# Pieces of 384 tokens, joined rows of array tiles and blocks of 1024 tokens in a two-stage feed-forward kernel on one core

## The chip, the cores and the metric

The kernel runs on one core of one Trainium2 chip. The metric is the device time of one execution in microseconds (us), and the time of a kernel is the median of its runs.

## The reference, cut to what matters

Eight batches of 576 tokens, 8 heads of 64. A packed attention (32 learned queries read the keys and values, then the tokens read the 32 results) gives x of 4608 x 512. Two feed-forwards follow, all in float32.

```python
p_packed = sm_attn(p, k, v)                 # 32 rows per head
out = sm_attn(q, p_packed, p_packed)        # 576 rows per head
x = out.transpose(0, 2, 1, 3).reshape(4608, 512)
h = x @ w_in                                # 512 x 2048
x = (h * sigmoid(1.702 * h)) @ w_out        # 2048 x 512
h = max(x @ w1, x @ w2, x @ w3)             # 512 x 768 each
return h @ w_out2                           # 768 x 512
```

## The kernel before

**Precision.** Every large product is made of three matmuls (`mm3`, lines 111 to 115): each operand is kept as a high and a low part of the reduced type fp32r, and low x high, high x low and high x high are added up in one PSUM bank. Each of the three has weights of its own to load.

**First feed-forward.** For a batch and a group of four heads, the second attention product and `w_in` are put together: `pw_unit` multiplies the 32 packed rows of each head with their rows of `w_in`, so that h is the attention weights `at` times `pw`. These are matmuls of 64 rows by 32 columns, 8 of which stand in the array side by side; in float32 each is issued as two instructions, so a row of one group (g) for two batches is 16 instructions on line 460. The two results go through the two banks of `ps_a`, and ScalarE and VectorE split them into high and low parts (lines 146 and 147). The work is then cut into units: 288 tokens (half a batch, `HALF`) by 128 of the 2048 inner columns (`fc`). `h_unit` has 2 x 3 matmuls into one of the two banks of `ps_h`, then the activation; `g_unit` splits the result; `out_unit` has 4 x 3 matmuls that are summed over `fc` in the four banks of `ps_c`. A batch half takes 16 units, then its result goes to `x2d` in DRAM. Batches 0 and 1 take their halves in turns of 4 and 8 columns (`PAT`), with partial sums kept in SBUF; of the other batches only the last does (chunks of 4).

**Second feed-forward.** Six blocks of 768 tokens. A 2 x 2 block product with seven multiplications (Strassen's form) is made for each of nine weight sets (three weights, three pairs of column blocks): `Set.steps` has seven products of 2 x 3 matmuls with 384 columns, and VectorE adds them up and takes the maximum. The sums of x (T1 to T4) and their splits are made once a block by `x_steps`, from what `x_loads` brings; the weight sets come from DRAM with two loads each (`load_set`, lines 664 and 665, issued on POOL), where earlier steps (`Piece`) have put them. `out2` then multiplies by the last weights: 18 matmuls of 512 columns for 128 tokens.

**Order.** `main` writes down a due time for every step (`add`), sorted into one program order. The framework then orders the instructions of each engine by that order and by when their operands and buffers are ready. `tn[n]` is the due time of unit n; `pw_unit` of a pair of batches stands `Q_` or `R_` units ahead of its first use. Buffers come from pools: 16 large ones (`wp`, tag "w") for weights, x and weight sets, and 4 (tag "x") for the first feed-forward's results and the reloaded `w_in` parts (`load_wi`).

## Time and profile before

| | us |
|---|---|
| median of 3 runs | 1297.01 |
| lowest and highest run | 1295.29, 1297.29 |
| the profiled execution | 1295.06 |
| its span, first to last instruction | 1293.3 |
| TensorE busy in the span | 1272.8 (98%) |
| VectorE, ScalarE, POOL busy | 841.8, 522.7, 78.2 |
| moved by DMA | 233.07 MB |

All times inside the kernel are those of the one profiled execution. Matmuls overlap each other, so the busy time of a group of matmuls counts parts of the span more than once, and the distance between two starts is what one of them takes. A line in square brackets behind an instruction tells how long its engine had been idle and what released it.

### The profile page before, as it was taken

The numbers are of one execution on the slowest core, as the hardware profiler recorded it, in microseconds if no ns is written. First come the engines' busy times: TensorE is split into PE (matmuls) and PEld (weight loads), VectorE is DVE, ScalarE is ACT, GpSimd is POOL, SyncE is SP. The second block draws the span as 40 slices with busy tenths as digits, with TensorE's granted clock in tenths as the row PEclk, the third lists the DMA queues.
The fourth block names the chain that finished last, engine by engine and source line by source line (L and its number), as shares of the span: only waits on it lengthen the run. The fifth ranks groups of instructions, "written<-read, shape, count | busy, mean of one in ns | idle before, by whom it ended". The sixth has DMA issues, their size and how long they took to land.

```text
span 1293.3 us, 24741 instructions
## 1 busy us (share of the span) xinstructions
PE 1272.8 (98%) x9990; PEld 1179.7 (91%) x9990; DVE 841.8 (65%) x1734; ACT 522.7 (40%) x1133; POOL 78.2 (6%) x153
## 2 busy tenths in 40 slices
PE   6999999999999999999999999999999999999998
PEld 5688888899989899999999999899899999998997
DVE  7998788565543466588789887557467366366561
ACT  3676654454654454455556532312213123113111
POOL 1000000000000000000000011011011011010100
PEclk8999999999999999999999999999999999999999
DMA  8898254323220231045557399567477477474541
GB/s 311 315 406 314 74 157 145 103 88 99 91 87 18 90 109 48 24 145 182 170 180 240 129 347 342 202 218 245 157 260 250 156 260 247 160 254 177 187 172 49
DMA packets 84402, 233.07 MB, mean 180 GB/s; under 512 B 9792, under 2 KB 38976, under 8 KB 77376
## 3 DMA queue, kind: packets, MB, share of 16 engines
q1 hardware_dynamic: 64128, 115.62, 26.0%
q0 software_dynamic: 20160, 115.88, 25.8%
q8 instruction: 78, 1.28, 0.4%
q14 instruction: 36, 0.29, 0.1%
HBM read 191.88 MB, written 39.58 MB: 179 GB/s over the span
## 4 chain that ended last, share of the span: by engine, by line
PE 88%; DVE 5%; DMA 3%; ACT 2%; issue 1%; SPq 0%; DVEq 0%; ACTq 0%
PE p L115 10%; PE p L114 10%; PE p L113 10%; PE acc L113 10%; PE acc L115 9%; PE acc L114 9%; PE h L113 5%; PE h L115 4%; PE h L114 4%; PE accb L115 4%; PE accb L114 4%; PE accb L113 4%; PE pw L460 2%; PE s L311 1%; DMA wraw_o<-in_w_out 1%; PE pv L366 1%
## 5 line engine op out<-in xcount | busy, mean ns | idle before, releaser
L113 PE MATMUL acc<-g,wo 128*128 128x288 f32 x1024 | 309.0, 302 | 1.9 <-DVE x L559 1.4
L115 PE MATMUL acc<-g,wo 128*128 128x288 f32 x1024 | 301.1, 294 | 0.0
L114 PE MATMUL acc<-g,wo 128*128 128x288 f32 x1024 | 299.4, 292 | 0.0
L113 PEld LDWEIGHTS acc<-g,wo 128*128 128x128 f32 x1024 | 192.2, 188 | 32.3 <-ACT t L526 11.9
L115 PEld LDWEIGHTS acc<-g,wo 128*128 128x128 f32 x1024 | 192.0, 188 | 1.4 <-issue 1.3
L114 PEld LDWEIGHTS acc<-g,wo 128*128 128x128 f32 x1024 | 192.3, 188 | 0.6 <-issue 0.5
L113 PE MATMUL h<-at,pw 128*128 128x288 f32 x512 | 154.0, 301 | 1.2 <-ACT at L142 0.6
L114 PE MATMUL h<-at,pw 128*128 128x288 f32 x512 | 151.5, 296 | 0.4 <-DVE at L143 0.4
L115 PE MATMUL h<-at,pw 128*128 128x288 f32 x512 | 151.3, 296 | 0.0
L113 PE MATMUL p<-x_T,ws 128*128 128x384 f32 x324 | 108.2, 334 | 0.0
L114 PE MATMUL p<-x_T,ws 128*128 128x384 f32 x324 | 108.2, 334 | 0.0
L115 PE MATMUL p<-x_T,ws 128*128 128x384 f32 x324 | 108.1, 334 | 0.0
L750 DVE TENSOR_TENSOR u<-s,p 128x384 f32<-128x384 f32 x54 | 29.9, 554 | 118.3 <-PE p L115 118.3
L113 PEld LDWEIGHTS h<-at,pw 128*128 128x128 f32 x512 | 96.1, 188 | 9.7 <-issue 5.0
L534 DVE TENSOR_TENSOR g<-t,g 128x288 fp32r<-128x288 f32 x130 | 58.9, 454 | 67.9 <-ACT g L533 67.0
L524 ACT ACTIVATE t<-h 128x288 f32<-128x288 f32 x130 | 53.3, 410 | 112.5 <-PE h L115 112.1
L114 PEld LDWEIGHTS h<-at,pw 128*128 128x128 f32 x512 | 96.1, 188 | 1.6 <-DVE t L527 0.8
L115 PEld LDWEIGHTS h<-at,pw 128*128 128x128 f32 x512 | 96.1, 188 | 0.5 <-issue 0.5
L780 ACT COPY s<-p 128x384 f32<-128x384 f32 x54 | 25.9, 480 | 164.5 <-PE p L115 164.5
L527 DVE SCALAR_TENSOR_TENSOR t<-t,h 128x288 f32<-128x288 f32 x126 | 56.8, 451 | 54.1 <-ACT t L526 53.4
L526 ACT ACTIVATE t<-h 128x288 f32<-128x288 f32 x126 | 51.8, 411 | 93.2 <-PE h L115 92.7
L115 PE MATMUL accb<-wo,g 128*128 128x512 f32 x216 | 84.1, 390 | 0.0
(166 smaller groups left out, 2587.7 us busy)
## 6 DMA issues: line engine op xcount, KB each, us to landing
ws<-wss POOLq DMA_DIRECT2D x54, 1024.0 KB, 7.5
wa<-wsa POOLq DMA_DIRECT2D x54, 768.0 KB, 4.6
wi<-wsc POOLq DMA_DIRECT2D x24, 512.0 KB, 3.7
k<-in_k SPq DMA_DIRECT2D x16, 576.0 KB, 4.0
q<-in_q SPq DMA_DIRECT2D x16, 576.0 KB, 4.1
x2d<-x SPq DMA_DIRECT2D x16, 576.0 KB, 3.6
wss<-ws SPq DMA_DIRECT2D x36, 256.0 KB, 2.9
xr<-x2d SPq DMA_DIRECT2D x24, 384.0 KB, 4.3
```

The lines of the kernel that those rows point to most:

```text
L113: nc.tensor.matmul(o, al, bh, start=start, stop=False, skip_group_check=more)
L114: nc.tensor.matmul(o, ah, bl, start=False, stop=False, skip_group_check=more)
L115: nc.tensor.matmul(o, ah, bh, start=False, stop=stop, skip_group_check=more)
L311: self.mm = nc.tensor.matmul(o[hf][rows(c, r, hf ^ self.swap), :HALF], w(c, rows_in(r)), x[rows_in(r), c, hf * HALF:hf * HALF + HALF], sta ...
L366: self.mm = nc.tensor.matmul(o[h][m, :D], self.et[rows_in(h), c * P + NP * j:c * P + NP * j + NP], self.v[rows_in(h), c, d:d + D], start=c ...
L460: nc.tensor.matmul(os[b][rows(x, r, b & 1)], sp[b, g][rows_in(r), NP * c:NP * c + NP], w[rows_in(r), c], start=True, stop=True,)
L524: latest["act"] = nc.scalar.activation(t, o, AF.Gelu_apprx_sigmoid)
L526: nc.scalar.activation(t, o, AF.Tanh, scale=0.5 * 1.702)
L527: nc.vector.scalar_tensor_tensor(out=t, in0=t, scalar=1.0, in1=o, op0=ALU.add, op1=ALU.mult)
L534: latest["dve"] = nc.vector.tensor_tensor(out=g[:, 1], in0=gt[n], in1=f(g[:, 0]), op=ALU.subtract)
L750: latest["dve"] = nc.vector.tensor_tensor(out=o, in0=a, in1=b, op=op)
L780: latest["act"] = nc.scalar.copy(self.s1, self.b1)
```

## The change

In the first feed-forward, batches 2 to 7 are taken as one run of 3456 tokens in 9 pieces of 384. A piece may lie across two batches; its `h_unit` then computes h in two parts of 192 columns. The last two pieces are interleaved in chunks of four inner column blocks. The result of a piece is stored in two halves. The rows of both groups are computed one directly behind the other (`pw_both`), the second into the banks of `ps_h`, and the output unit of the piece before is moved from behind the next `h_unit` to directly behind the rows. Where this happens follows from the due times (three pairs of batches 0 and 1 and all twelve of batches 2 to 7).

The second feed-forward takes three blocks of 1024 tokens and two of 768, so a product has 512 or 384 columns. For blocks after the first, `x_loads` and `x_steps` run twice, for one half of the rows (k) each, through smaller buffers. A third of the weight sets from number 11 on have buffers of their own, sets 2 to 10 are loaded one set later than before, a third of the split results g moves to the large buffers, and there are fewer m, t and g buffers. The tables of due times are replaced.

```diff
-BT = 768
-HT = BT // 2
-NBLK = NT // BT
+HTS = [512, 512, 512, 384, 384]
+HT = max(HTS)
+NBLK = len(HTS)
+C0 = [2 * sum(HTS[:j]) for j in range(NBLK)]
+WIDE = 384
...
-T_ = [41.76, 1.21, 1.17, 7]
+T_ = [40.26, 1.21, 1.17, 10]
...
-    def pw_unit(bs, pr, g, n):
+    def pw_unit(bs, pr, g, n, tile_=pa_tile):
...
-            os[b] = pa_tile(f"pw_{b}_{g}_{n}")
+            os[b] = tile_(f"pw_{b}_{g}_{n}")
...
+        return lambda: pw_out(os, g, n)
...
+    def pw_both(bs, pr, n):
+        for done in [pw_unit(bs, pr, g, n, (pa_tile, h_tile)[g]) for g in range(2)]:
+            done()
...
+    runs = [(x, 0, NFC) for x in range(2 * S, NT, WIDE)]
+    runs[-2:] = [(x, y, y + 4) for y in range(0, NFC, 4) for x in range(NT - 2 * WIDE, NT, WIDE)]
...
     def h_unit(n):
...
+        for b, t0, num, to in parts:
+            for g in range(2):
+                w = pw[b, fc // 4][:, g]
+                mm3(
+                    o[:, to:to + num], (w[:, 0, fs], w[:, 1, fs]), [t[:, t0:t0 + num] for t in at[b, g]],
+                    g == 0, g == 1, len(parts) > 1,
+                )
...
     def load_set(n):
...
+        if n > 9 and n % 3 == 2:
+            a = late["x"].tile([P, 12 * P], F32R, tag="wa", name=f"wa_{n}")
+            s_ = late["x"].tile([P, 16 * P], F32R, tag="ws", name=f"ws_{n}")
...
-                st[key] = f_tile("m", 8, f"m_{self.n}_{c}")
+                st[key] = f_tile("m", 6, f"m_{self.n}_{c}", self.ht)
...
+                add(tn[nn] + hu[nn] / 2 + .02, pw_both, (2 * pr, 2 * pr + 1), pr, n)
+                early.add(nn - 1)
+
+        for n in range(N1):
+            add(tn[n], h_unit, n)
+            add(tn[n + 1] + hu[n + 1] / 2 + .03 if n in early else tn[n + 2] + hu[n + 2] / 2, out_unit, n)
+            add(tn[n] + hu[n] / 2 + .01, g_unit, n)
...
+            elif n < 11:
+                add(max(ts[n - 2] + DS[0] * 6 / 7 + .1, saved.get(n, 0)), load_set, n)
             else:
                 add(ts[n - 2] + .1, load_set, n)
...
-                add(t0 - 14, x_loads, j + 1)
-                for dt, fn in x_steps():
-                    add(t0 + 1 + 1.5 * dt, fn)
+                add(t0 - 14, x_loads, j + 1, 0)
+                add(t0 + .9, use_x, j + 1)
+                for dt, fn in x_steps(0):
+                    add(t0 + 1 + E_[0] * dt, fn)
+                add(t0 + 1 + E_[0] * 9.1, open_raw, j + 1, 1)
+                add(t0 + 1 + E_[0] * 9.1 + .1, x_loads, j + 1, 1)
+                for dt, fn in x_steps(1):
+                    add(t0 + E_[1] * DO[j] + E_[0] * dt, fn)
```

## Rows read from the trace of the kernel before

**Rows 1.** The page's head: span, busy time and share of each engine

```profile
span 1293.3 us, 24741 instructions
PE 1272.8 (98%) x9990; PEld 1179.7 (91%) x9990; DVE 841.8 (65%) x1734; ACT 522.7 (40%) x1133; POOL 78.2 (6%) x153
```

**Rows 2.** Busy by stage: stretch, length, engines (instructions), clock, DMA share, GB/s

```profile
260.00:620.00 360.00, 359.95 (x3495) 332.09 (x3494) 210.21 (x486) 181.45 (x431) 7.55 (x14) 1.00 0.28 91
620.00:749.00 129.00, 128.39 (x972) 127.94 (x971) 108.33 (x244) 73.24 (x160) 2.70 (x5) 1.00 0.53 178
749.00:1293.30 544.30, 540.67 (x2919) 514.85 (x2917) 314.38 (x576) 124.45 (x223) 55.53 (x103) 1.00 0.62 217
```

**Rows 3.** Timeline of TensorE (start, duration, instruction): first and last of 361 matmuls

```profile
623.67 0.30 PE L113 MATMUL h<-at,pw 128*128 128x288 f32 x1
...
671.15 0.30 PE L113 MATMUL h<-at,pw 128*128 128x288 f32 x1
```

**Rows 4.** The same timeline, second feed-forward: ends of 43 matmuls, then of 87

```profile
1020.38 0.33 PE L113 MATMUL p<-x_T,ws 128*128 128x384 f32 x1
...
1027.66 0.33 PE L113 MATMUL p<-x_T,ws 128*128 128x384 f32 x1
...
1269.79 0.39 PE L113 MATMUL accb<-wo,g 128*128 128x512 f32 x1
...
1289.29 0.39 PE L115 MATMUL accb<-wo,g 128*128 128x512 f32 x1
```

**Rows 5.** Groups by line: count | busy us, mean ns | idle before

```profile
L460 PE MATMUL pw<-wi,sp 64*32 64x512 f32 x384 | 26.1, 601 | 0.0
```

**Rows 6.** Timeline of the weight loads behind a pair of 64-column matmuls

```profile
291.84 0.32 PEld L383 LDWEIGHTS ptp<-fold,pn 128*128 128x128 f32 x2
292.08 0.19 PEld L113 LDWEIGHTS acc<-g,wo 128*128 128x128 f32 x1
292.19 0.19 PEld L114 LDWEIGHTS acc<-g,wo 128*128 128x128 f32 x1
```

**Rows 7.** Timeline of TensorE around one row of array tiles

```profile
353.81 0.29 PE L115 MATMUL h<-at,pw 128*128 128x288 f32 x1
354.02 1.09 PE L460 MATMUL pw<-wi,sp 64*32 64x512 f32 x16
355.04 0.41 PE L113 MATMUL acc<-g,wo 128*128 128x288 f32 x1
355.28 0.29 PE L114 MATMUL acc<-g,wo 128*128 128x288 f32 x1
```

**Rows 8.** Timeline of TensorE, two rows of batches 0 and 1

```profile
120.00 1.09 PE L460 MATMUL pw<-low_wi,sp 64*32 64x512 f32 x16
...
123.69 1.68 PE L460 MATMUL pw<-low_wi,sp 64*32 64x512 f32 x16 [0.82 <-DVE pw L147]
```

**Rows 9.** Timelines of VectorE and TensorE: emptying behind the row of 354.02, behind another

```profile
355.81 1.29 DVE L147 TENSOR_TENSOR pw<-pw,pw 128x512 fp32r<-128x512 f32 x2 [0.31 <-ACT pw L146]
...
616.20 1.09 PE L460 MATMUL pw<-wi,sp 64*32 64x512 f32 x16
...
619.49 1.28 DVE L147 TENSOR_TENSOR pw<-pw,pw 128x512 fp32r<-128x512 f32 x2
```

**Rows 10.** Groups by line and shape, VectorE

```profile
L750 DVE TENSOR_TENSOR m<-t,m 128x384 f32<-128x384 f32 x108 | 59.5, 555 | 2.3
L626 DVE TENSOR_TENSOR c<-c,wa 128x512 f32<-128x512 f32 x18 | 12.3, 685 | 0.0
```

**Rows 11.** POOL's timeline, one set; issues of 740 to 780: KB, median landing

```profile
770.51 0.55 POOL L664 DMA_DIRECT2D wa<-wsa  x1 [5.70 <-PE p L115]
771.55 0.54 POOL L665 DMA_DIRECT2D ws<-wss  x1 [0.49 <-PE p L115]
...
ws<-wss POOLq DMA_DIRECT2D x5, 1024.0 KB, 9.1
```

**Rows 12.** Timeline of TensorE at the start of the first feed-forward

```profile
42.37 0.40 PE L114 MATMUL h<-at,pw 128*128 128x288 f32 x1 [0.42 <-DVE at L143]
```

More of the change, by code (lines that the diff above doesn't have):

```diff
@@ L530, in g_unit @@
     def g_unit(n):
-        g = gp.tile([P, 2, HALF], F32R, tag="g", name=f"g_{n}")
+        g = gp.tile([P, 2, WIDE], F32R, tag="g", name=f"g_{n}")[:, :, :units[n][0][1]]
         if direct(n):
@@ L542, in out_unit @@
     def out_unit(n):
-        b, hf, fc = units[n]
+        (c0, width, _), fc = units[n]
         w = wo[fc]
@@ L554, in out_unit @@
             if dc == 0:
[L555 to L557 removed]
+                old = part.pop(c0, None)
+                num = KD if width == HALF else 2
+                x2 = old or [
+                    x_tile(f"x2_{n}_{y}")[:, :num * width].rearrange("p (c t) -> p c t", c=num)
+                    for y in range(KD // num)
+                ]
+            to = x2[dc // num][:, dc % num]
             if old is not None:
[L559 to L569 removed]
+                nc.vector.tensor_tensor(out=to, in0=o, in1=to, op=ALU.add)
+            elif dc % 2 == 0 or c0 < 2 * S:
+                nc.scalar.copy(to, o)
+            else:
+                nc.vector.tensor_copy(to, o)
+            if fc == NFC - 1 and dc % num == num - 1:
+                nc.sync.dma_start(x2d[:, dc + 1 - num:dc + 1, c0:c0 + width], x2[dc // num])
+        if n in last and fc < NFC - 1:
+            part[c0] = x2
     wo2, xs, xv, st = {}, {}, {}, {}
     ws = {}
+    xt = {}
     nps = [0]
+    gw = {}
     def c_tile(name):
@@ L770, in put @@
                 fc, hf = self.p + c // 2 * 3, c % 2
-                g = late["f"].tile([P, 2, HT], F32R, tag="g", bufs=12, name=f"g2_{self.n}_{c}")
+                if self.p == 0:
+                    if (self.j, fc) not in gw:
+                        gw[self.j, fc] = w_tile(f"g2_{self.n}_{fc}")
+                    g = gw[self.j, fc][:, hf, :, :self.ht]
+                else:
+                    g = late["f"].tile([P, 2, HT], F32R, tag="g", bufs=8, name=f"g2_{self.n}_{c}")[:, :, :self.ht]
                 nc.scalar.copy(g[:, 0], m)
@@ L883, in main @@
         attention(A_[3], 1, 1, AS_[3], 0)
-        N1 = 2 * B * NFC
+        N1 = len(units)
         tn = [0.0] * 300
+        early = set()
         t = T0
+        hu = [HU * (units[min(n, N1 - 1)][0][1] / HALF) for n in range(N1 + 2)]
         for n in range(N1 + 2):
             tn[n] = t
-            if n < N1:
-                add(t, h_unit, n)
-            if n >= 2:
-                add(t + HU / 2, out_unit, n - 2)
-            if n < N1:
-                add(t + HU / 2 + .01, g_unit, n)
-            t += (T_[1] * HU) if n < T_[3] else HU * T_[2]
+            t += hu[n] * (T_[1] if n < T_[3] else T_[2])
         TB0 = t
```

257 lines of the change are left out of this document (135 added, 122 removed).

## The prediction

> **What bounds the kernel now.** I read the page's head first: TensorE is busy in 1272.8 of 1293.3 us, every other engine below two thirds [rows 1]. The same engine by stage comes next [rows 2]: from 260 us to the end it is never free for more than 0.7 us in a stage until the tail, at the full clock (2.4 GHz). So in those stages nothing but the matmuls' own time counts, and a wait on another engine is a loss only if the change makes one. The price of a matmul is then not its busy time (they overlap) but the distance between starts. In a stretch without interruption the first feed-forward takes 47.48 us for 20 units of 18 matmuls of 288 columns, 131.9 ns each [rows 3]. The second takes 7.28 us for 42 matmuls of 384 columns, 173.3 ns, and 19.50 us for 86 of 512, 226.7 ns [rows 4]. At 2.4 columns per ns that is 120 + 11.9, 160 + 13.3 and 213.3 + 13.3. So what wider pieces can save is about 13 ns for each matmul that disappears.
>
> The sum is made against the profiled execution, 1295.06 us (span 1293.3 and 1.76 around it). That is 1.95 below the median of 1297.01, so what comes out is shifted by 1.95 at the end.
>
> **Wide pieces in the first feed-forward.** Batches 2 to 7 have 192 units of 18 matmuls: 3456 x 131.9 = 455.8 us. After, the same 3456 tokens are 9 pieces of 384, 144 units. Six pieces lie in one batch: 96 x 18 x 173.3 = 299.5. Three straddle two batches, and there h is computed in two halves of 192 columns, because each batch has weights of its own: 48 x 12 matmuls of 384 for the output, 99.8, and 48 x 12 = 576 of 192 for h. No matmul of 192 columns of this type is in the trace. From below it costs 80 + 13.3 = 93.3 ns, by the two wider shapes; from above 131.9, the nearest shape. What chooses is the weight load, since every one of these matmuls has its own 128x128 weights. The trace shows it uncovered at one place only: behind a pair of 64-column matmuls the starts of the following loads stand 0.11 us apart, though there is little to stream [rows 6]. The two loads of the first row (0.32 us with a last load of 0.19) start at 291.84 and 291.97; the next at 292.08 and 292.19: 0.11 and 0.11. The two other instances that I read, at 203 and 269 us, give the same, with a mean of 0.111. I take 0.111, since that is the load itself: 63.9 us. Sum 463.3 against 455.8: **+7.5 us**, between -2.7 (93.3 ns) and +19.5 (131.9). The wide pieces cost more at the seams than they save.
>
> The Trainium skill ("TensorE: Matmul & The Clock Gate", Back-to-back issue gap) puts the distance of warm matmuls at N/2.4 + 2.5 ns, which the rows here exceed by about 10 ns at every width; by it both forms would be within 1.5 us of each other, and the seams would be free. The same page's section on LDWEIGHTS has the load at columns/1.2, 107 ns for 128, which would make the seams 61.6 us; the rows side with that one.
>
> VectorE and ScalarE get fewer and longer instructions per token, and they are off the path. The last two pieces run interleaved in chunks of four, as batch 7 did.
>
> **Rows of array tiles.** The weights of two batches (pw) are now made for both groups in one go, 32 instead of 16 instructions. One row costs, from the matmul before to the second one after it, 355.28 - 353.81 = 1.47, less two matmul slots of 0.13: 1.21 us [rows 7]. The instruction lasts 0.60 us at 512 columns [rows 5] against 0.39 for the same width in the feed-forward [rows 4]: 0.21 longer, which is another 512 columns at 2.4 per ns, so these stream at half rate, 0.427 us, on 8 tiles: 0.85 for 16 instructions. The other 0.36 is paid for changing the array's form and back, once per row. Twelve merged pairs in batches 2 to 7 save 12 x 0.36 = 4.4 us. Of batches 0 and 1 three pairs are merged; there the rows also waited for their banks, as at 123.69 [rows 8]. The six rows cost 9.9 us in all by the same measure; 3 x 2.07 with a stall of 0.4 each is 7.4: -2.5.
>
> The new wait: the second group writes into the two banks of h, so the next h waits until ScalarE and VectorE have emptied them. Two tiles are empty 3.07 us after the row's start at best, at 0.64 each (355.81 + 1.29, less 354.02) [rows 9]; the third, which frees the first h bank, at 3.71. TensorE is done with the long row at 1.98 (it went on 1.13 after the short one's start, 0.85 are added) and has the output unit that was moved there in front of the next h, 12 x 173.3 = 2.08: 4.06. So in the clean case it is hidden. Where other work is queued on the two engines it isn't: at 616.20 the second tile was empty only after 4.57 (619.49 + 1.28) [rows 9], 1.5 later. Of the 24 rows in batches 2 to 7, 7 are late by 0.8 us or more. Behind the waiting h stand the next h and all output units; nobody else waits. Cost between 0 and 5 us (four pairs at 1.2); I take 2.5. The two loads of group weights that a joined row needs go out together, 10 and 8 units ahead, on POOL, which has nothing else to issue then; they share four buffers with the pieces' results, and a pair that gets its buffer late moves its row, which I cost at 0. Together **-4.4 us**.
>
> **Second feed-forward.** A set is 42 matmuls. Six blocks of 9 sets at 384 are 2268 x 173.3 = 393.1 us. After: 27 sets at 512, 1134 x 226.7 = 257.1, and 18 at 384, 131.0: 388.1. **-5.0 us**. The output part (36 tiles) keeps its matmuls. What has to stay hidden: in a last set of three VectorE has 13 instructions, 13 x 0.685 (the 512-wide row) = 8.9 in 9.52 us, where it had 13 x 0.555 = 7.2 in 7.28 [rows 10]; so cover is no thinner. The x sums come in two rounds of 11 VectorE instructions, 15.1 us, and a reload between them, within 8 x 18 x 226.7 ns = 32.6 us of output work (12.2 in 24.5 for the short blocks). SP has the second round's loads ahead of some output stores; those wait for VectorE's first round, which leaves the output copies half of the stage, and I cost it at 0. Weight sets 2 to 10 are now asked for one set ahead (9.52 us) instead of two: POOL issues the second load 1.0 us behind the first, it lands in 9.1 at this stage [rows 11], and its first reader runs 9.52 + 1.36 (one product of 6) = 10.9 after the release. 0.8 us of margin: cost 0, and up to 1 us a set if it is gone. The handover between the stages holds weights of two batches to the end of the first feed-forward, so x and set 0 get their buffers one chunk (8 units) later; I cost it at 0, at most 3 us.
>
> **Start.** Unit 0 waits for batch 0's attention until 42.37 [rows 12]; by the due times it is placed 1.5 us sooner and group 1's loads go first. The bounds are -3 and +2; I take **-1.5**.
>
> Sum: 7.5 - 4.4 - 5.0 - 1.5 = -3.4: 1291.7 for the profiled execution, **1293.6** as a median, 0.26% faster.
>
> **The rivals.** *Free seams*: the 192-column matmul costs 93.3 ns, the weight load being hidden there too. For it: at 288 columns loads do follow at 131.9 without showing. Against: rows 6. It gives 10.2 less: 1283.4. *Bank wait (slower)*: the third tile is late at most of the 15 places. If all are as at 616 us, third release 5.2 against 4.06, it is 15 x 1.15 = 17 instead of 2.5: 1308. It decides from a mean wait of 0.65 us, with which the total passes 1299.6. For it: 7 of 24 rows of before are late enough. Against: their places are moved. The skill warns of just this ("TensorEngine Tiling (Array Packing)", PSUM Bottleneck: packing speeds up TensorE but not the emptying of PSUM); the late rows agree. *Rows not joined*: the order that is issued follows readiness, and at 120.00 and 123.69 two rows that the code gives one after the other ran 3.7 us apart [rows 8]. Then the 4.4 are lost: 1298.0. *Late sets*: 9 sets x 1 us: 1302. *Half rate*: the narrow matmuls fall to the rate of rows 5, 173.3 ns: +36, 1329.5; nothing narrow contradicts it, no wide one supports it.
>
> **How the numbers follow.** Forecast 0.43, free seams 0.15, bank wait 0.20, not joined 0.10, late sets 0.08, half rate 0.04. About 0.2% (2.6 us) is what can be told from no change, so faster is below 1294.4: 0.33 of the forecast, all of free seams, 0.04 of others, 0.52. Slower (above 1299.6): 0.14 of bank wait, half rate, 0.04 of late sets, 0.22. The rest, 0.26, is within. The range goes from free seams with no bank wait (1281) to a bank wait of 0.9 us (1303), leaving half rate and the worst bank wait out. The forecast alone is 1288 to 1298.
>
> **What would show it.** The distance of the 192-column starts: 0.11, or 0.093, or 0.173. A straddling unit should take 3.4 us, a plain wide one 3.12. The rows of 32 should show one form change, and h behind them an idle time released by the pw evacuation. The second feed-forward should show 226.7 ns and no idle time at sets 2 to 10 or at the handover. I am wrong if the seams are cheap, if the two rows run apart, or if idle time sits behind them in most places.

## The result and the profile after

| | before | after |
|---|---|---|
| median, us | 1296.37 | 1307.22 |
| lowest and highest run | 1295.29, 1297.29 | 1306.72, 1308.32 |
| the profiled execution | 1295.06 | 1307.14 |
| first feed-forward ends (first product `p`) | 749.12 | 763.84 |
| last matmul ends | 1289.68 | 1301.40 |

The ratio of the runs on one chip is 1.0085 (95% interval 1.0068 to 1.0103). The change makes the kernel 0.85% slower; the forecast was 0.26% faster, and 1307.2 lies above its range. The head of the page and the busy time by stage, which answer to [rows 1, 2]; the columns are those of rows 2, with the boundary of the stages moved to 763.84:

```profile
span 1305.4 us, 22517 instructions
PE 1277.5 (98%) x9036; PEld 1141.9 (87%) x9036; DVE 835.0 (64%) x1618; ACT 510.2 (39%) x1032; POOL 68.3 (5%) x135
```

```profile
260.00:620.00 360.00, 359.54 (x3085) 332.43 (x3091) 203.55 (x430) 172.32 (x360) 8.63 (x16) 1.00 0.28 90
620.00:763.84 143.84, 138.07 (x864) 136.03 (x849) 116.61 (x238) 72.78 (x138) 2.70 (x5) 0.99 0.51 172
763.84:1305.40 541.56, 536.52 (x2539) 465.35 (x2538) 309.31 (x532) 122.88 (x221) 45.84 (x85) 1.00 0.55 187
```

The loss is not in the middle of the first feed-forward, where TensorE is as busy as it was. It is in its last stretch: 5.8 us free between 620 and 763.84, where before had 0.6, and a clock below 1.00. The matmuls' own prices first, in the timeline of TensorE (start, duration): six matmuls of 192 columns, one plain unit of 384 from its first h to the next unit's, a joined row with its neighbours, and a set of 512 columns from one product to the same product of the next set.

```profile
707.58 0.27 PE L121 MATMUL h<-at,pw 128*128 128x192 f32 x1
...
708.14 0.27 PE L123 MATMUL h<-at,pw 128*128 128x192 f32 x1
...
666.77 0.33 PE L121 MATMUL h<-at,pw 128*128 128x384 f32 x1
...
669.89 0.33 PE L121 MATMUL h<-at,pw 128*128 128x384 f32 x1
...
413.67 0.34 PE L123 MATMUL acc<-g,wo 128*128 128x384 f32 x1
413.94 1.95 PE L468 MATMUL pw<-wi,sp 64*32 64x512 f32 x32
415.81 0.44 PE L121 MATMUL acc<-g,wo 128*128 128x384 f32 x1
416.09 0.33 PE L122 MATMUL acc<-g,wo 128*128 128x384 f32 x1
...
890.60 0.39 PE L121 MATMUL p<-x_T,wa 128*128 128x512 f32 x1
...
900.12 0.39 PE L121 MATMUL p<-x_T,wa 128*128 128x512 f32 x1
```

Every price of the sum is there, as in [rows 3, 4, 7]: 0.56/5 = 0.112 for 192 columns (the mean of all such distances is 0.1110), 3.12/18 = 0.1733 for 384, 416.09 - 413.67 - 2 x 0.1733 = 2.07 for a joined row (2.07 was worked out), 9.52/42 = 0.2267 for 512. Now the stretch that nobody priced. VectorE's timeline, TensorE's, and the busy time of two stretches behind it (the granted clock stands behind POOL's column):

```profile
709.84 0.43 DVE L615 TENSOR_SCALAR c_o<-wraw_o 128x512 int32<-128x512 int32 x1 [1.15 <-DMA wraw_o<-in_w_out]
...
712.66 1.94 DVE L586 TENSOR_TENSOR x<-acc,x 128x384 f32<-128x384 f32 x4
...
713.36 0.66 PE L121 MATMUL acc<-g,wo 128*128 128x384 f32 x1 [4.95 <-DVE x L586]
```

```profile
713.30:716.70 3.40, 3.34 (x11) 3.37 (x12) 3.40 (x7) 1.04 (x3) 0.00 (x0) 0.50 0.69 249
716.80:718.00 1.20, 1.20 (x12) 1.20 (x11) 0.97 (x3) 0.00 (x0) 0.00 (x0) 1.00 0.98 227
```

After the last 192-column matmul at 708.14 TensorE has nothing to do until 713.36: the output unit needs the four output banks, and the four adds (L586) that bring the interleaved pieces' partial sums out of them stand in VectorE's queue behind conversions (L615 to L624) of the second feed-forward's last weights (`conv_wo2`), one of which waits for its raw weights. Behind the 4.95 us the clock is granted at 0.50, half of full speed (1.2 GHz), until 716.7, and at 1.00 again from 716.8. The twelve matmuls of this output unit take 3.71 us (713.36 to the next h at 717.07) where 12 x 0.1733 = 2.08 is their price: 1.6 us more. With the 5.1 us in front of them, 6.7 of the last stretch's loss stand at this one place.

For a balance, the price by its width was taken from every distance between starts of TensorE's timeline; what is left over goes to the rows, waits and other work. The waits of h behind the rows stand in the line of the other gaps.

| part | forecast | found, after less before |
|---|---|---|
| start, to the first output matmul | -1.5 | +1.6 (48.86 to 50.50) |
| first feed-forward, matmul slots | +7.5 | +7.5 (605.4 to 612.9) |
| rows of array tiles, with the wait before them | -4.4 | -4.5 (39.1 to 34.6) |
| attention's rows and transposes between units | 0 | +3.9 |
| other gaps up to 630 us | 0 | -1.4 |
| idle time and half clock from 630 us on | 0 | +7.7 (1.2 to 8.9) |
| second feed-forward | -5.0 | -3.0 (540.6 to 537.6) |
| sum | -3.4 | +11.8 |

### The profile page after: what moved, and what is told of

It is laid out like the page before. It is cut to its first block, busy times and chain, and to the rows that moved or that the text cites. A ratio compares the mean times of both kernels' runs of the same rounds, so it can differ in the third digit from the quotient of the medians.

```text
span 1305.4 us, 22517 instructions
## 1 busy us (share of the span) xinstructions
PE 1277.5 (98%) x9036; PEld 1141.9 (87%) x9036; DVE 835.0 (64%) x1618; ACT 510.2 (39%) x1032; POOL 68.3 (5%) x135
## 4 chain that ended last, share of the span: by engine, by line
PE 84%; DVE 7%; issue 3%; ACT 3%; DMA 2%; SPq 0%; POOL 0%; POOLq 0%; ACTq 0%; DVEq 0%
PE acc L121 9%; PE p L121 9%; PE p L122 9%; PE p L123 9%; PE acc L123 9%; PE acc L122 9%; PE h L121 5%; PE h L122 5%; PE h L123 5%; PE accb L123 4%; PE accb L121 4%; PE accb L122 4%; PE pw L468 2%; PE s L319 2%; PE pv L374 1%
## 5 line engine op out<-in xcount | busy, mean ns | idle before, releaser
L121 PE MATMUL acc<-g,wo 128*128 128x384 f32 (+1 forms) x832 | 273.0, 330 | 6.1 <-DVE x L586 5.2
L123 PE MATMUL acc<-g,wo 128*128 128x384 f32 (+1 forms) x832 | 268.8, 324 | 0.0
L122 PE MATMUL acc<-g,wo 128*128 128x384 f32 (+1 forms) x832 | 268.7, 323 | 0.0
L121 PEld LDWEIGHTS acc<-g,wo 128*128 128x128 f32 x832 | 156.1, 188 | 24.8 <-issue 10.1
L121 PE MATMUL h<-at,pw 128*128 128x384 f32 (+2 forms) x512 | 157.5, 308 | 2.8 <-ACT at L150 1.8
L122 PEld LDWEIGHTS acc<-g,wo 128*128 128x128 f32 x832 | 156.9, 189 | 1.7 <-DVE g L557 1.1
L123 PEld LDWEIGHTS acc<-g,wo 128*128 128x128 f32 x832 | 156.6, 188 | 0.1
L122 PE MATMUL h<-at,pw 128*128 128x384 f32 (+2 forms) x512 | 155.5, 304 | 0.0
L123 PE MATMUL h<-at,pw 128*128 128x384 f32 (+2 forms) x512 | 155.1, 303 | 0.0
L121 PEld LDWEIGHTS h<-at,pw 128*128 128x128 f32 x512 | 96.8, 189 | 13.7 <-issue 6.2
L121 PE MATMUL p<-x_T,ws 128*128 128x512 f32 (+1 forms) x270 | 99.4, 368 | 1.0 <-DMA ws<-wss 1.0
L550 DVE SCALAR_TENSOR_TENSOR t<-t,h 128x384 f32<-128x384 f32 (+1 forms) x112 | 57.2, 512 | 66.8 <-ACT t L549 66.4
L122 PE MATMUL p<-x_T,ws 128*128 128x512 f32 (+1 forms) x270 | 99.3, 368 | 0.0
L123 PE MATMUL p<-x_T,ws 128*128 128x512 f32 (+1 forms) x270 | 99.0, 367 | 0.0
L122 PEld LDWEIGHTS h<-at,pw 128*128 128x128 f32 x512 | 97.2, 190 | 1.3 <-DVE at L151 0.8
L123 PEld LDWEIGHTS h<-at,pw 128*128 128x128 f32 x512 | 97.3, 190 | 0.0
L785 DVE TENSOR_TENSOR u<-s,p 128x512 f32<-128x512 f32 (+1 forms) x45 | 28.5, 634 | 106.6 <-PE p L123 106.3
L549 ACT ACTIVATE t<-h 128x384 f32<-128x384 f32 (+1 forms) x112 | 51.5, 461 | 106.5 <-PE h L123 105.9
L557 DVE TENSOR_TENSOR g<-t,g 128x384 fp32r<-128x384 f32 (+1 forms) x96 | 50.8, 530 | 61.8 <-ACT g L556 61.6
L121 PE MATMUL accb<-wo,g 128*128 128x512 f32 x216 | 84.1, 389 | 0.0
L123 PE MATMUL accb<-wo,g 128*128 128x512 f32 x216 | 84.0, 389 | 0.0
L122 PE MATMUL accb<-wo,g 128*128 128x512 f32 x216 | 84.0, 389 | 0.0
```

What stands on the lines that cost most here:

```text
L121: nc.tensor.matmul(o, al, bh, start=start, stop=False, skip_group_check=more)
L122: nc.tensor.matmul(o, ah, bl, start=False, stop=False, skip_group_check=more)
L123: nc.tensor.matmul(o, ah, bh, start=False, stop=stop, skip_group_check=more)
L549: nc.scalar.activation(t, o, AF.Tanh, scale=0.5 * 1.702)
L550: nc.vector.scalar_tensor_tensor(out=t, in0=t, scalar=1.0, in1=o, op0=ALU.add, op1=ALU.mult)
L557: latest["dve"] = nc.vector.tensor_tensor(out=g[:, 1], in0=gt[n], in1=f(g[:, 0]), op=ALU.subtract)
```

## The experiments

All against the kernel before on the same chip. "Ends" is the start of the first product `p`, "second" the time from there to the last matmul's end. Times inside a kernel are those of its one profiled execution, which can lie up to 3 us from its median.

| kernel | median | ratio (95%) | ends | second |
|---|---|---|---|---|
| before | 1296.4 | | 749.1 | 540.6 |
| changed | 1307.2 | 1.0085 (1.0068 to 1.0103) | 763.8 | 537.6 |
| e1 pieces of 288, joined rows | 1297.9 | 1.0015 (1.0005 to 1.0026) | 754.8 | 539.4 |
| e2 pieces of 288, rows apart | 1295.6 | 0.9995 (0.9984 to 1.0006) | 751.0 | 538.8 |
| e3 no seams | 1290.0 | 0.9959 (0.9945 to 0.9972) | 736.0 | 546.4 |
| e4 adds first | 1308.6 | 1.0096 (1.0083 to 1.0109) | 760.8 | 542.7 |
| e6 light last weights | 1314.6 | 1.0146 (1.0132 to 1.0159) | 772.9 | 536.3 |
| e7 small first block | 1309.2 | 1.0101 (1.0087 to 1.0114) | 763.7 | 541.1 |
| e8 rows apart | 1314.2 | 1.0143 (1.0127 to 1.0158) | 770.2 | 537.5 |
| e9 as e2, small first block | 1298.0 | 1.0012 (1.0004 to 1.0021) | 749.8 | 543.3 |
| e10 loads on POOL | 1307.8 | 1.0093 (1.0079 to 1.0108) | 767.5 | 537.3 |
| e11 as e2, loads on POOL | 1294.3 | 0.9981 (0.9972 to 0.9990) | 747.5 | 540.1 |
| e12 as e11, joined rows, other leads | 1297.1 | 0.9999 (0.9988 to 1.0010) | 755.4 | 539.1 |
| e13 four raw buffers | 1303.9 | 1.0063 (1.0049 to 1.0076) | 761.6 | 536.8 |
| e14 two raw buffers | 1328.3 | 1.0248 (1.0234 to 1.0262) | 785.2 | 537.5 |
| e15 as e11, four raw buffers | 1293.6 | 0.9988 (0.9979 to 0.9997) | 747.5 | 539.4 |
| e16 four raw buffers, POOL | 1303.8 | 1.0062 (1.0048 to 1.0075) | 760.3 | 536.9 |
| e17 four raw buffers, adds first | 1308.5 | 1.0100 (1.0086 to 1.0113) | 759.9 | 542.2 |
| e18 as e11, joined rows, banks swapped | 1289.1 | 0.9946 (0.9932 to 0.9959) | 745.8 | 539.8 |

### The seams: e5, e3

```diff
+    for width in (64, 96, ..., 512):
+        run(f"full{width}_", width, P, 36)    # 36 matmuls, 128 weight columns each
+    for width in (64, ..., 256):
+        run(f"half{width}_", width, D, 36)    # 64 weight columns
```

> Not the computation at all: rows of 36 matmuls of one width each, all of the same type as in the feed-forwards, first with 128 columns of weights (widths 64 to 512; each matmul loads its own weights), then with 64 columns of weights (widths 64 to 256). The distance between starts is read. Theory (a matmul of this type takes its columns at 2.4 per ns plus 12 to 13 ns, but never less than its weight load): with 128 columns of weights 0.111 us flat at 64 to 224 columns, then 0.119 at 256, 0.132 at 288, 0.146 at 320, 0.173 at 384, 0.200 at 448 and 0.227 at 512; with 64 columns of weights half the floor, about 0.055 at 64 and 96, 0.066 at 128, 0.080 at 160, 0.093 at 192. Rival (the 0.111 of the straddling pieces comes from their place, with three weights for two streams, or from a half rate for narrow streams): 192 columns at 0.093 here, or at 0.16.

TensorE's timeline (one line is a row of 36), then its busy time and clock in stretches:

```profile
27.64 7.89 PE L88 MATMUL full__201<-x 128*128 128x96 f32 x36
35.33 7.90 PE L88 MATMUL full__238<-x 128*128 128x128 f32 x36
...
57.56 4.19 PE L88 MATMUL full__349<-x 128*128 128x208 f32 x36
61.59 4.19 PE L88 MATMUL full__386<-x 128*128 128x224 f32 x36
65.62 4.20 PE L88 MATMUL full__423<-x 128*128 128x240 f32 x36
69.66 4.48 PE L88 MATMUL full__460<-x 128*128 128x256 f32 x36
73.97 4.90 PE L88 MATMUL full__497<-x 128*128 128x288 f32 x36
...
117.59 3.35 PE L88 MATMUL half__843<-x 128*64 128x192 f32 x36
120.78 3.87 PE L88 MATMUL half__880<-x 128*64 128x224 f32 x36
```

```profile
27.64:50.74 23.10, 23.10 (x109) 23.10 (x110) 0.00 (x0) 0.00 (x0) 0.00 (x0) 0.50 0.03 11
57.56:105.87 48.31, 48.31 (x326) 46.19 (x325) 0.00 (x0) 0.00 (x0) 0.00 (x0) 1.00 0.00 1
```

Start to start, divided by 36: 0.1119 us at 208 and at 224 columns, 0.1122 at 240, 0.1197 at 256, so there is a floor of 0.112. With 64 weight columns 192 columns take 3.19/36 = 0.0886. The floor belongs to the weight load, as the first theory has it. The row of 192 columns with 128 weight columns ran mostly at half clock; its last eight distances, after the clock had risen, have a mean of 0.111, so 192 columns lie on the floor here too. The Trainium skill ("TensorE: Matmul & The Clock Gate", LDWEIGHTS) puts a load at its columns/1.2, which is 107 ns for 128, near the 111 to 112 found. The N/2.4 + 2.5 ns that the Trainium skill gives for a single matmul (same page, Back-to-back issue gap) is exceeded by 9 ns here at 288 columns. The rows at 96 and 128 columns take about twice the floor because the clock was at half then, which is taken up at the end.

```diff
         parts = []
...
+        if len(parts) > 1:
+            parts = [(parts[0][0], S - width, width, 0)]
```

> The changed kernel, but a piece that lies across two batches takes 384 tokens of its first batch alone (its h is one group of 6 matmuls of 384 columns instead of 12 of 192, so these tokens' results are not the reference's). Theory (weight load bounds the narrow matmuls at 0.111 us): 48 x (12 x 111.0 - 6 x 173.3 ns) = 14.0 us less than the changed kernel. Rival (narrow ones cost 93.3 ns and the loss is elsewhere): 3.8 us less.

The straddling pieces take 384 columns of one batch here. 17.2 us less than the changed kernel: the first feed-forward ends 27.8 sooner, and the second lasts 8.8 longer. Of the 27.8, 14.0 are the seams by the prices above (576 x 0.1110 - 288 x 0.1733), 8.9 are the idle time and half clock of the handover, of which 0.01 is left here, and 3.5 are 20 matmuls of the first feed-forward that now run behind the first products. These 3.5 lengthen the second stage again, and 5.4 of the handover's gain come back as waits and half clock in its first block, the longest of them behind VectorE:

```profile
752.93 0.80 PE L121 MATMUL p<-x_B,ws 128*128 128x512 f32 x1 [3.50 <-DVE m L788]
```

So the seams cost what was forecast, and the change without them gains, but not by their price alone: the handover's idle time went with them. That says something of its cause. e3 has the changed kernel's due times, and its VectorE is busier in front of the handover, 19.85 of 20 us:

```profile
680.00:700.00 20.00, 20.00 (x118) 20.00 (x117) 19.85 (x47) 11.41 (x22) 0.00 (x0) 1.00 0.69 216
```

The changed kernel has 18.04 there and 17.47 in the next 20 us, yet in e3 TensorE never waits for the adds. In e3 two conversions of last weights start between two groups of four adds, 12.9 us apart (677.79 and 690.66); in the changed kernel four do, 20.2 apart (692.47 and 712.66). So neither VectorE's load nor the due times alone decide, but the order that comes out; what turned it is not shown. And what is saved in front of the first block is partly paid inside it.

### New blocks and joined rows with pieces of 288: e1, e2

```diff
-WIDE = 384
+WIDE = 288          # e1, e2; and the due-time tables of before
...
-add(..., pw_both, (2 * pr, 2 * pr + 1), pr, n)
+for g in range(2):  # e2 only
+    add(..., pw_one, (2 * pr, 2 * pr + 1), pr, g, n)
```

> The changed kernel with pieces of 288 tokens again and the due-time tables of before; the joined rows and the blocks of 1024 stay. Theory (seams and handover made the loss): no matmul of 192 columns, no idle time of 5 us at the chunk change, so rows (-5 to -7 us) and blocks (-2.8 to -5) are left: 1285 to 1290 where before is 1296. Rival (joined rows cost more than they save, by the h banks): 1296 or above, with idle time of TensorE behind the rows. Rival (blocks of 1024 cost, by late weight sets): second feed-forward longer than 540 us.

> As e1, with the rows of the two groups apart, placed and loaded as before: before with the new blocks alone. Theory: 3 us faster than before by the blocks (537 to 538 us for the second feed-forward instead of 540.4), so e1 is 5 to 7 us faster than this. Rival (joined rows lose): this is as fast as e1 or faster.

The new blocks alone leave the time where it was (e2, 0.9995), which is less than was expected of them. Their matmul slots do fall by 5.0 us (540.0 to 535.0), but 2.9 us of waits stand in the first block, and 0.4 more than before in the rest and 0.6 more in front of it; 1.2 more stand at the start. Joined rows, which the sum credits with 4.4 us, lose 2.3 here (1297.9 against 1295.6). In e1's profile two things take more than the rows save: one row breaks into three pieces behind ScalarE (4.64 us from 434.25 on, instead of 2.07), and h waits behind the rows, about 0.15 us behind each of eight and 1.80 behind one:

```profile
616.81 0.40 PE L121 MATMUL h<-at,pw 128*128 128x288 f32 x1 [1.80 <-DVE pw L155]
```

The waits of h are the rival called bank wait. The next three runs ask when it decides.

### Joined rows: e8, e12, e18

```diff
 # e8: the changed kernel with pw_one for g = 0, 1 as in e2
 # e12, e18: pieces of 288, rows joined, raw weights' loads on POOL
-R_ = [18, 26, 14, 8]
+R_ = [19, 32, 16, 11]                  # e12, e18
+Q_ = [8, 11, 9, 9]                     # e12; e18 keeps 9, 8, 9, 8
...
-pw_unit(bs, pr, g, n, (pa_tile, h_tile)[g])
+pw_unit(bs, pr, g, n, (h_tile, pa_tile)[g])   # e18 only
```

> The changed kernel with the rows of array tiles as before: 16 instructions for one group, its own weight load, into the projections' own banks; everything else as changed. Theory (a joined row costs 2.08 us where two single ones cost 2 x 1.22, and with the changed kernel's placements hardly any h waits for a bank): 15 x 0.36 = 5.4 us lost, 1311 to 1313. Rival (as with 576-token batches in halves of 288, where joined rows lost 2.3 us): 1304 to 1306.

> As the run before it in this list (pieces of 288 tokens, new blocks, raw weights' loads on POOL), but with joined rows of array tiles, their leads in units scaled from the changed kernel's (units of 384 tokens) to units of 288: 19, 32, 16 and 11 units ahead from batch 4 on instead of 18, 26, 14 and 8. With the leads of before, joined rows lost 2.3 us (one row broken by waits took 4.64 us instead of 2.08, one h waited 1.8 us for its bank). Theory (a joined row gains wherever neither wait arises; the changed kernel's rows gained 7.0 us): 4 to 6 us less than the same kernel with rows apart, 1287 to 1289. Rival (at pieces of 288 tokens the two output units that cover the emptying of the banks are too short, so h waits in most places): no less than with rows apart.

> Pieces of 288 tokens, new blocks, raw weights' loads on POOL, joined rows with the first group's results in the two banks of h and the second's in the projections' banks (the other way round before), leads 9, 8, 9, 8 and 19, 32, 16, 11 units. With the banks as in the change a joined row cost 2.33 us here (0.16 of it the next h waiting for the third tile to be emptied, 2.4 at one place). Theory (the h banks are now emptied first, 1.3 us sooner than the third tile was): that wait goes, a joined row costs 2.1 us in the clean places, and the kernel takes 3 to 5 us less than with rows apart: 1289.5 to 1291.5. Rival (the row now waits at its start for h's banks, which ScalarE has just to empty): 1293 to 1297.

e8 takes 7.0 us more than the changed kernel. With rows apart the time of all rows and the waits before them is 41.6 us, with joined ones 34.6. So here the step was right in sign, and worth more than the 5.4 expected, because some rows that stand apart also waited in these places (one takes 2.38 us with its wait and three others 1.7 to 2.2, where a clean one takes 1.11).

e12 takes the time of before, 2.8 us more than e11. The same row in its VectorE's and TensorE's timelines, then one of e12's bad places:

```profile
553.01 1.95 PE L468 MATMUL pw<-wi,sp 64*32 64x512 f32 x32
554.79 2.48 DVE L155 TENSOR_TENSOR pw<-pw,pw 128x512 fp32r<-128x512 f32 x4 [1.32 <-ACT pw L154]
556.45 0.29 PE L123 MATMUL acc<-g,wo 128*128 128x288 f32 x1
556.73 0.40 PE L121 MATMUL h<-at,pw 128*128 128x288 f32 x1
...
588.25 0.61 PE L121 MATMUL h<-at,pw 128*128 128x288 f32 x1 [2.25 <-DVE pw L155]
```

The four tiles are emptied 0.60 apart from 554.79, the third by 556.67, which is 3.66 after the row's start; the prediction worked out 3.71. The output unit covers only 12 x 0.132 after the row, and the last of it starts at 556.45: h could follow at 556.58 and starts at 556.73. This 0.15 stands at seven of the twelve rows alone, makes such a row 2.33 (with the slower first matmul behind a wait) against 2 x 1.22, and leaves no slack where VectorE has other work (2.25). With 384 columns the cover is 4.06 and the wait is gone. e12 also lost 3.1 us inside one row that waited for its weights (`wi`), which its early leads asked for too late.

e18 gives the first two tiles to the banks that h needs. Its row at the same work:

```profile
547.99 1.95 PE L468 MATMUL pw<-wi,sp 64*32 64x512 f32 x32
...
551.42 0.29 PE L123 MATMUL acc<-g,wo 128*128 128x288 f32 x1
551.56 0.29 PE L121 MATMUL h<-at,pw 128*128 128x288 f32 x1
```

h follows after 0.14, a normal distance. Ten of the twelve rows cost 2.07 to 2.08, the others 2.21 and 2.48: 25.4 us in all, where e11's 24 single rows cost 29.4. The comparison is cleanest in the eight rows of batches 4 to 7, where e12 has the same leads: behind them h waits 3.7 us in all in e12 and 0.0 in e18. The theory holds: 1289.05 us, 0.9946 (0.9932 to 0.9959), 4.5 us less than e11 by the two ratios. It beats before and the changed kernel, and has the joined rows and the new blocks but no wide pieces.

### The idle time at the handover: e4, e6, e7, e10

```diff
+        with tc.issue_after(latest["dve"].ins):     # e4: conversions behind the latest add
             conv_late(f"o{fc}", wo2[fc], w[:, 0], w[:, 1], TB)
...
-HTS = [512, 512, 512, 384, 384]
+HTS = [384, 512, 512, 512, 384]                     # e7; sets 2 to 10 asked for two ahead
...
-        nc.sync.dma_start(raw, w_out2[fc])
+        nc.gpsimd.dma_start(raw, w_out2[fc])        # e10; the three loads of a Piece too
```

(e6 puts one ScalarE copy and one VectorE subtraction in the place of `conv_late` for these six tiles.)

> The changed kernel, with the conversions of the last weights ordered on VectorE behind the additions of the partial sums that precede them in the plan; the work is the same. Theory (the idle 5 us at 708 are VectorE's conversions and their wait for a DMA ahead of the additions that free the banks, and the half clock behind it costs 1.8): 6 to 7 us less than the changed kernel, and no clock dip. Rival (the DMA itself or the large buffers are the bound): the idle time stays or moves behind, less than 2 us gained.

> The changed kernel, but the six tiles of the second feed-forward's output weights are converted with one VectorE and one ScalarE instruction each instead of six and two; the exact conversion of these weights is left out. This takes about 2.6 us of VectorE work per tile, 16 us in all, out of the stretch in which the changed kernel's TensorE waited 4.95 us for the partial sums of the last pieces (708 to 713 us). Theory (VectorE is the engine that is late over the whole handover, from the last pieces to the first sets of the second feed-forward): the 5 us of idle time and the half clock behind it go, 6 to 8 us, and the first block gets no longer; 1299 to 1301 in all. Rival (what is late is the chain of buffers and transfers into the first block, x through DRAM and the weight sets): the first feed-forward ends 6 to 8 us sooner, but the first block waits 4 to 7 us longer, as it did when the seams or the order of the adds were changed; 1304 to 1307.

> The changed kernel with the blocks of the second feed-forward as 768, 1024, 1024, 1024 and 768 tokens instead of 1024 x 3 and 768 x 2, and weight sets 2 to 10 asked for two sets ahead where their buffers are free. Matmuls are the same, 388.1 us of products. Theory (the handover is late because the first block's operands are a third larger: 11 VectorE instructions of 1.22 us instead of 0.9, and larger transfers): the idle time in front of and inside the first block falls from 10.5 us (8.9 before it, 1.6 in it) to 2 to 4 us, 1299 to 1301 in all. Rival (the size has no part in it; VectorE's backlog of weight conversions and the four adds of the last pieces decide): the 4.95 us stay, 1306 to 1308. Second rival: the sets of 7.28 us outrun the weight loads in the first block, 1 to 2 us at each of up to 8 sets, 1309 to 1320.

> The changed kernel with the loads of the raw weights of the second feed-forward (18 pieces of three transfers, 6 tiles of the output weights) issued by POOL, which issues nothing from 561 to 734 us, instead of SP, where they stand behind the stores of the converted weights (SP waited 29 us for those between 650 and 760 us). Theory (SP's queue makes the raw weights late, VectorE's queue waits with their conversion, and the adds of the last pieces and TensorE behind it): the 4.95 us of idle time before the adds fall below 1 us, with the half clock behind them; 6 us less in front of the second feed-forward, 2 to 3 of them lost again in its first block; 1303 to 1304. Rival (the ring of three raw buffers and the order of VectorE's instructions decide, whichever queue asks): the idle time stays at 4 to 7 us, 1306 to 1308.

None gains. In e4 the idle time at 713 is gone, so the adds' place in VectorE's queue is what made it; but it moves. Its first feed-forward ends 3.1 us sooner and the second lasts 5.1 longer (1.4 of it are 8 matmuls of the first that run behind the first products). Its TensorE, at the next adds and in the first set:

```profile
750.24 0.41 PE L121 MATMUL acc<-g,wo 128*128 128x384 f32 x1 [2.59 <-DVE x L586]
...
771.24 0.50 PE L121 MATMUL p<-x_B,wa 128*128 128x512 f32 x1 [2.06 <-ACT s L821]
```

e6 has 12 us less work on VectorE (823.0 busy instead of 835.0; 16 were expected) and waits longer, 7.17 us before the adds and 3.81 at 693.88, and so neither theory for it holds: the work alone isn't the cause, and the first block did not get longer (536.3). What it waits for is seen on ScalarE, which copies the raw weights there:

```profile
688.06 0.65 ACT L686 CAST wo<-wraw_o 128x512 fp32r<-128x512 f32 x1 [4.74 <-DMA wraw_o<-in_w_out]
```

e7 waits 5.10 us at the same place, so the size of the first block is not the cause; besides, its sets of 7.28 us outrun two weight loads (1.8 and 1.1 us). e9, which is e2 with the blocks of e7, was to give 1290 to 1292 and gives 1298.0: its sets outrun the loads too (2.25 and 0.66 us), and its first block still waits 1.79 us behind VectorE, though it is as small as before's. The waits stand in the first block and not, as its rival has it, at the second.

> The kernel before with the second feed-forward in blocks of 768, 1024, 1024, 1024 and 768 tokens: pieces of 288 tokens, rows apart, the first block as large as before, weight sets 2 to 10 asked for two sets ahead where their buffers are free. Theory (the larger blocks save 5.0 us of matmul slots, and what took it back was the larger first block at the handover, 1.9 us in front of it and 2.9 in it): the handover is that of before, 5 us less than before, 1290 to 1292, faster than both. Rival (the cost belongs to the two-round loading of x and to the buffers of the larger operands, wherever the first large block stands): 1294 to 1297, the waits standing at the second block.

e10 waits 6.53 us, but it shows what holds the loads, since POOL issues nothing but them in that stretch. POOL's timeline, VectorE's, TensorE's:

```profile
703.78 0.53 POOL L678 DMA_DIRECT2D wraw_o<-in_w_out  x1 [2.50 <-DVE wa L624]
706.49 0.53 POOL L678 DMA_DIRECT2D wraw_o<-in_w_out  x1 [2.19 <-DVE wo L624]
...
710.24 0.43 DVE L615 TENSOR_SCALAR c_o<-wraw_o 128x512 int32<-128x512 int32 x1 [2.85 <-DMA wraw_o<-in_w_out]
...
717.24 0.66 PE L121 MATMUL acc<-g,wo 128*128 128x384 f32 x1 [6.53 <-DVE x L586]
```

A load of raw weights goes out as soon as VectorE has read (L624) an earlier tile of the three raw buffers, lands 3.7 us later, and VectorE then waits for it, with the adds behind. It is a ring of three buffers with VectorE on both ends.

### The ring and the order: e13, e14, e16, e17

```diff
-raw = late["r"].tile([P, 2 * TB], I32, tag="raw", bufs=3, ...)
+raw = late["r"].tile([P, 2 * TB], I32, tag="raw", bufs=4, ...)   # e14: 2
-                t = f_tile("t", 2, f"t_{self.n}_{c}", self.ht)
+                t = f_tile("t", 1, f"t_{self.n}_{c}", self.ht)   # makes the room; not in e14
```

> The changed kernel with four buffers for raw weights of the second feed-forward instead of three (the room comes from one of two buffers of a VectorE-only intermediate in that stage). Theory (the three buffers are the cause of the idle time before the adds: a raw load waits until VectorE has converted the tile three before it, VectorE then waits for that load, and the adds stand behind): a load has one conversion more, some 3.5 us, of lead; the 4.95 us fall to 0 to 2, with the half clock behind them; 4 to 6 us less in front of the second feed-forward, some of it given back in the first block: 1302 to 1304. Rival (the order of VectorE's instructions alone: five conversions stand in front of the four adds whether their data are there or not): 4 us or more of idle time, 1306 to 1308.

> The changed kernel with two buffers for raw weights instead of three. Theory (the ring sets the pace): every load of 4 to 5 us is then bare at the handover, the idle time before the adds grows from 5 to 8 us or more, and the first block starts later: 1311 to 1320. Rival (order alone): within 2 us of the changed kernel, 1305 to 1309.

> The changed kernel with four buffers for raw weights and their loads issued by POOL. With POOL alone the idle time was 6.5 us, POOL's loads waiting for the last reader of the tile three before. Theory (ring, with SP's queue second): less than with either alone, idle time below 1 us, 1300 to 1303. Rival (order alone): 1306 to 1308.

> The changed kernel with four raw buffers and, on VectorE, the conversions of the output weights issued behind the latest adds of the last pieces. Four buffers alone left 3.6 us of idle time with VectorE busy without a break from 694 to 711 us; the order alone moved the idle time to 747 us and ScalarE's set stage. Theory (the two causes are the ring and the order, and each alone only moves the rest): less than 2 us of idle time in front of the second feed-forward, 2 to 4 us less than with four buffers alone: 1300 to 1302. Rival (VectorE's total work between 690 and 760 us is too much in any order): the idle time moves again, 1303 to 1307.

With two buffers the kernel loses 21 us more, beyond the 1311 to 1320 that were expected. VectorE's waits from 620 to 770 us in e14 (total, times, longest), which in the changed kernel are 4.5 and 1.1 us:

```profile
DVE c L615 <- DMA wraw<-in_w: 20.6, 7, 6.2
DVE c_o L615 <- DMA wraw_o<-in_w_out: 10.7, 4, 5.7
```

With four, VectorE waits for no load at all in that stretch, and 3.3 us are gained. But 3.57 us of idle time stay, and now it is the order alone: VectorE is busy 16.66 of the 16.80 us before the adds, and half free 10 us later. e13, busy by stretch, then TensorE:

```profile
694.00:710.80 16.80, 13.96 (x94) 13.79 (x92) 16.66 (x40) 8.39 (x16) 0.00 (x0) 1.00 0.70 238
720.00:740.00 20.00, 20.00 (x130) 20.00 (x129) 10.53 (x20) 8.48 (x18) 1.08 (x2) 1.00 0.27 86
740.00:760.00 20.00, 20.00 (x120) 19.75 (x119) 18.85 (x27) 12.45 (x20) 1.26 (x3) 1.00 0.44 154
```

```profile
711.54 0.66 PE L121 MATMUL acc<-g,wo 128*128 128x384 f32 x1 [3.57 <-DVE x L586]
```

So both theories hold a part: the ring some 1.4 us of the idle time (4.95 to 3.57), and, as e4 has it, the order the rest. POOL on top (e16) changes nothing, against its theory. e17, with both remedies, has VectorE evenly at 14.6 to 15.0 of 20 us from 680 to 740, but now conversions and sums of x stand in front of and between the adds at 749: TensorE waits 2.57 and 0.82 us for them, and 2.06 us in the first set. The idle time moved, as its rival says, though not by the amount of work: VectorE is busy 18.6 of 20 us from 740 to 760, and in e13 18.85 without such a wait. e17 has put some of the conversions into the half-free stretch of 720 to 740; an order that has all of them done there was not tried, and whether it frees both ends stays open.

### The loads on POOL with pieces of 288: e11, e15

> The kernel before with the new blocks of the second feed-forward (1024 x 3, 768 x 2), pieces of 288 tokens, rows apart, and the raw weights' loads on POOL. Without the last step it took the time of before: 5.0 us of matmul slots saved, 4.7 lost at the handover and in the first block. Theory (SP's queue): 2 to 3 of the 4.7 us come back, 1292.5 to 1293.5. Rival (ring and order): 1295 to 1297.

> The kernel before with the new blocks, the raw weights' loads on POOL and four raw buffers. Without the fourth buffer it was faster than before by 0.19% and had no idle time left in front of the second feed-forward, but 4.2 us in its first block (1.6 behind VectorE, 1.7 behind weight sets). Theory (earlier conversions also end earlier, so the first block's operands and sets are earlier): 1.5 to 3 us less, 1291 to 1293. Rival (the first block waits for buffers that only the last pieces free): no difference, 1293.5 to 1295.

With pieces of 288 the handover's idle time vanishes with POOL alone (0.06 us of gaps from 630 us on, where e2 has 1.8). e11 gains 0.19% on before; 1294.3 lies between its theory and its rival. 4.2 us stay in the first block in e11, 3.5 in e15, whose ratio can't be told from e11's: there the ring isn't what is late, as its rival says.

## Why the prediction was wrong

**Wide pieces: right.** +7.5 was forecast and +7.5 is found, by 0.111 at the seam. The rivals with free seams and at half rate are excluded by e5 and by the after trace. It was also the plainest warning: a part that costs 7.5 us has to be paid for by the others, and they had only 10.9 to give. (Two sums among the rivals are off by about 1 us: a mean bank wait of 0.9 at 15 places gives 1304.6, not 1303, and 1299.6 is passed from 0.57. The measured 1307.2 lies above either.)

**Joined rows: right, and for the reason given.** The row costs 2.07; h waits for its bank only 0.9 us in all, where 2.5 were taken, since a row's emptying hides behind the moved output unit of 384 columns. (One of the three pairs of batches 0 and 1 ran broken up by other work, in four pieces from 74 to 86 us.) The working that gave 3.71 against 4.06 also tells why the same step loses with 288 (3.66 against 3.56), and how to mend it (e18). With the warning of the Trainium skill ("TensorEngine Tiling (Array Packing)", PSUM Bottleneck: the emptying of PSUM does not get faster with the packed matmuls) the 2.25 us of e12 agree; in the changed kernel it is the 0.9.

**The handover: the step that failed.** "x and set 0 get their buffers one chunk (8 units) later; I cost it at 0, at most 3 us" looks at the wrong wait. It was 7.7 us in front of the second feed-forward, 6.7 of them through VectorE's queue: the adds of the last two pieces behind weight conversions, a ring of three raw buffers, and the half clock behind the idle time. The sentence "VectorE and ScalarE get fewer and longer instructions per token, and they are off the path" is the fault in it. On average it is so (116.6 of 143.8 us), but the last pieces' adds are on the path, and what stands ahead of them in VectorE's queue decides. That queue came out differently in the changed kernel; whether by the new due times, the wider pieces or their seams no run separates, and e3 has the new due times without the wait. The trace of before had the sign of it, in a line that the prediction did not use:

```profile
722.91 0.37 PE L113 MATMUL acc<-g,wo 128*128 128x288 f32 x1 [0.61 <-DVE x L559]
```

VectorE was not less busy in before: 18.46 and 19.17 of 20 us in the two stretches from 680 to 720, where the changed kernel has 18.04 and 17.47.

**The second feed-forward: mis-sized.** The matmul term is right, -5.0. The "0.8 us of margin" of the weight sets was too thin at two sets: TensorE waited 0.73 and 0.31 us for `ws`, and 1.6 in all were lost in the first block, 0.4 elsewhere. With pieces of 288 the first block lost more, 2.9 to 4.2 us in e1, e2 and e11. The new blocks gave 3.0 us in the changed kernel's second stage, and 0.5 to 1.8 with pieces of 288.

**The start: wrong, small.** Group 1's loads go first and unit 0 is due 1.5 us sooner, yet the first output matmul runs at 50.50, and at 49.5 to 52.1 in the other kernels with the new tables, against 48.3 to 51.1 with the old ones (before, e1, e2, e9, e11, e12, e15, e18). What is placed sooner still waits for batch 0's attention (1.81 us at 42.77, until ScalarE has made `at`). And something else stands there. TensorE's busy time in front of the first output matmul, in the changed kernel and in before:

```profile
44.32:47.73 3.41, 3.41 (x21) 3.25 (x20) 3.27 (x7) 3.09 (x8) 0.00 (x0) 0.50 1.00 384
...
37.84:48.86 11.02, 9.14 (x153) 6.30 (x153) 10.52 (x24) 7.72 (x20) 0.00 (x0) 1.00 0.92 358
```

The changed kernel works through 3.4 us here without a break at a granted clock of 0.50; by estimate that is up to 1.7 us, half of this stretch. Each of the eleven kernels with the new tables has such a stretch between 37 and 49 us, and none of the eight with the old ones has. No run was made for it. With the same tables the start spreads over 2.6 to 2.8 us, so the 1.6 of one execution is not exact: the means of the two groups are 50.5 and 49.6.

**Attention's rows: left out of the sum.** Some rows of s and t are broken up in other places, 3.9 us, with 1.4 gained in other gaps. No run was made for this alone, so that the new due times do it is argued; e1 and e2, with the old tables, have 6.5 and 6.2 us of s up to 230 us, the changed kernel 8.9.

So of the miss of 15 us (profiled executions; 13.6 by the medians), 7.7 are the handover, 3.1 the start, 2.5 the attention's rows with the other gaps, 2.0 the second feed-forward. Even with the handover as before the change would stand at about +4 us: the gains at the start and in the second feed-forward were priced too high, and the attention's rows had no price.

## What to carry to other kernels

Before giving an engine's work no price because it is free on average, look at each place where the busiest engine waits for what it makes, and at what is queued ahead there; an order that comes out differently is a change of its own. Time saved in front of a boundary is a gain only where the work behind it is ready too: of the 8.9 us that e3 saved at the handover, 5.4 came back. And when several short results must leave their banks, give the banks that are wanted next to those that are emptied first.

## What the runs showed of the hardware

With 128x128 weights of its own, a matmul of this type takes at least 0.111 to 0.112 us, up to 240 columns, and 0.0886 at 192 columns with 64 weight columns (e5, at a granted clock of 1.00). In e5 the granted clock fell from 1.00 to 0.50 (1.2 GHz) at about 26 us, within a row of 64-column matmuls that ran without a break; it stayed at 0.50 through the rows of 96, 128 and 160 columns (0.214 us for each matmul) and was back at 1.00 near the end of the row of 192. In the changed kernel, 192-column matmuls among wider ones ran at 1.00 (0.111 us). What made the difference was not tested. The pause of 5 us at the handover was followed by 0.50 from 713.3 to 716.7 and by 1.00 from 716.8.
